# Retention stage: ScalarE copies the state out of PSUM, and queries are loaded two pairs of tiles ahead

## The chip, the core and the metric

The kernel runs on one core of one Trainium2 chip. The metric is device time in microseconds (us) of one execution. The time before is 1370.45 us, the median of three runs (1362.09, 1370.45 and 1370.65).

## The reference, cut to what matters

Three layers follow one another. The change touches the first one only.

```
scores = (q @ k^T) / sqrt(64)                       # batch 8, 8 heads, 576 positions, head size 64
ret    = scores * gamma_h ** (i - j) for i >= j, else 0
x      = (ret @ v) as 4608 tokens x 512             # retention
x      = x + gate * relu(x @ w1[e]) @ w2[e]         # one of 8 experts per token, only where x @ w_skip > 0
out    = (P(x @ w_in) / Q(x @ w_in)) @ w_out        # gated polynomial layer
```

Scaling key j by gamma^-j and query i by gamma^i turns the decay into plain products. A causal sum can then be cut into tiles of 128 positions: inside a tile, masked scores times values; from earlier tiles, a running state, the sum of k^T v, times the queries.

## The kernel before

The 4608 tokens (8 sequences of 576) are cut into 36 tiles of 128. The retention stage is one loop over the tiles t = 0 to 35 (line 517), written inside a manual schedule: on each engine the instructions stand in the order in which the Python code issues them, and an engine's order is never changed by a scheduler.

Loads go through SP's queue. `load(t)` (line 251) brings keys (tile `lk`) and values (`lv`) of one tile, 0.26 MB each, four tiles ahead; their pools have five buffers. `load_q(c)` (line 265) brings the queries of two tiles, a pair c, 0.52 MB, as `lq`, in one DMA or, where the pair crosses from one sequence to the next, in two; `lq` has two buffers. Before the loop the kernel issues pairs 0 and 1 (lines 496 and 502); in the loop, at each even t, pair t/2 + 2 (line 531). At each even t SP also issues a 0.52 MB load of float64 weights (`c64`, printed as `c`, line 144), and at every t > 1 a store of one finished tile, `keep` (line 391, `Z<-xs`), which waits until ScalarE has copied `xs`. SP issues all of these in order and stops at the first one whose wait is not met.

GpSimd (POOL) scales the keys (`scale`, line 277, in place in `lk`) and the queries (`scale_q`, line 283: two instructions that read `lq` and write `qs`; `qs` has one buffer, which the transposes of the pair before must have read). It also sends list entries of routed tokens (line 456).

TensorE (PE) does, for tile t: both halves of `transp_q` for the next pair at even t (line 304, one half ahead of `scores(t + 1)`, one behind it), the masked scores of tile t + 1 (line 314), the transposes of the keys of tile t + 2 (`transp`, line 291), `outs(t)` (line 330: scores times values; line 335: state times queries), `state(t)` (line 352: the state grows by this tile in the PSUM tile `st`), and `rows(t - 1)` (line 373: transposition back and router logits).

After `state(t)` the running state is copied from PSUM to one of two SBUF tiles, `sms`, because the next tile's `outs` (line 335) uses it as weights. Two copies do it, one for each half of the partitions, 64 x 256 elements each:

```python
for e in range(2):
    r = slice(64 * e, 64 * e + 64)
    nc.vector.tensor_copy(out=x[r, :, r], in_=st[r])
```

There are 64 of them in the kernel (32 tiles, since the last tile of each group of nine needs none). In the loop they stand on VectorE (DVE) behind the score masks (line 320, tile `sm`) and, at even t, behind the seven or so instructions that turn float64 words into float32 (`conv_words`, `conv_lo`, lines 159 to 199).

ScalarE (ACT) copies the transposes (`tk` line 293, `tq` line 305), the outputs (`xt` line 338) and `xs` (line 377) out of PSUM, and does one step of the float64 conversion at even t (`conv_abs`, line 176, which waits for VectorE's line 159).

After the loop the routing lists are finished, and two stages follow, experts and the polynomial layer, which the change leaves as they are.

Of the kernel before, what the change touches and what calls it, by code (L numbers as in the profile page):

```python
# [21 lines left out]
NT = N // P  # L22
# [55 lines left out]
def body(nc, tc, a, out):  # L78
# [7 lines left out]
    Z = dram.tile([N, DM], F32, name="Z")  # L86
# [5 lines left out]
    ab = const.tile([P, 8], F32, name="ab")  # L92
    idx = const.tile([P, E, NC3, 2], I32, name="idx")

# [1 line left out]
    slots, raws = {}, {}  # L96
    pool = {"last": ctx.enter_context(tc.tile_pool(name="last", bufs=1))}
    win = [wi_p.tile([P, 2, 1024], F32R, name=f"wi{i}") for i in range(8)]
# [29 lines left out]
        w = slots[s]  # L128
        nc.vector.tensor_tensor(out=w[:, 1], in0=raws.pop(s), in1=w[:, 0].bitcast(F32), op=ALU.subtract)

    # float64 words to float32, rounded to nearest, and its two parts
    c64, cst8 = {}, {}
    NCA = 16
    items = [(0, 512 * n, 512) for n in range(NCA)]
# [64 lines left out]
            nc.vector.tensor_tensor(out=win[m][:, 1, o:o + W], in0=cst8.pop(n)[3],  # L199
                                    in1=win[m][:, 0, o:o + W].bitcast(F32), op=ALU.subtract)  # L200

# [1 line left out]
    at = ExitStack()  # L203
    pool["raw"] = at.enter_context(tc.tile_pool(name="raw", bufs=3))
    pool["cv"] = at.enter_context(tc.tile_pool(name="cv", bufs=2))
# [10 lines left out]
    def C(k):  # L216
        o, n = off[k]
        return cst[:, o:o + n]
# [11 lines left out]
    def setup():  # L230
        zero = rt_p.tile([P, E * RR * 2 // P], I32, tag="lp", name="zero", bufs=1)
        nc.vector.memset(zero, OOB)
        nc.sync.dma_start(out=XI.rearrange("(p r) c -> p (r c)", p=P), in_=zero)
        for p in range(NP):
            nc.sync.dma_start(out=iw[:, p, P:P + E], in_=a["moe_w_gate"][p * P:(p + 1) * P, :])
        nc.sync.dma_start(out=iw[:, :, P + E:P + E + 1],
                          in_=a["moe_w_skip"].rearrange("(c p o) -> p c o", p=P, o=1))
        nc.sync.dma_start(out=ab[:, 0:4], in_=a["moe2_a"].unsqueeze(0).to_broadcast([P, 4]))
        nc.sync.dma_start(out=ab[:, 4:6], in_=a["moe2_b"].unsqueeze(0).to_broadcast([P, 2]))
        nc.vector.tensor_copy(out=iw[:, :, 0:P], in_=ident.unsqueeze(1).to_broadcast([P, NP, P]))  # L240
        nc.vector.tensor_copy(out=upper, in_=C("upper"))
        nc.vector.memset(ones, 1.0)
        nc.vector.memset(ab[:, 6:7], 1.000001)
        nc.vector.memset(carry, 0.0)
        nc.vector.tensor_copy(out=ebase, in_=C("ebase"))
        nc.vector.tensor_copy(out=rowt[:, :, 0], in_=tok)
# [14 lines left out]
                nc.sync.dma_start(out=x[n:P], in_=src[b + 1, :, 0:P - n, :].rearrange("h p d -> p h d"))  # L261
            dst[t] = x

    # the queries of two tiles: two neighbours in a partition
    def load_q(c):
        b, s = divmod(2 * c * P, S)
        n = min(2 * P, S - s)
        x = ld_p.tile([P, H, 2, D], F32, tag="lq", name="lq", bufs=2)
        nc.sync.dma_start(out=x[0:n // 2], in_=a["q"][b, :, s:s + n, :].rearrange("h (p t) d -> p h (t d)", t=2))
        if n < 2 * P:  # L270
            nc.sync.dma_start(out=x[n // 2:P],
                              in_=a["q"][b + 1, :, 0:2 * P - n, :].rearrange("h (p t) d -> p h (t d)", t=2))
        lq[c] = x

    def scale(t, eng=nc.gpsimd):
        o = off["scale"][0] + (t % PER) * H
        eng.tensor_tensor(out=lk[t], in0=lk[t], in1=cst[:, o:o + H].unsqueeze(2).to_broadcast([P, H, D]), op=ALU.mult)

    def scale_q(c, eng=nc.gpsimd):
        o = off["scale"][0] + PER * H + (c % PER) * 2 * H  # L280
        x = ld_p.tile([P, 2, H, D], F32, tag="qs", name="qs", bufs=1)
        for i in range(2):
            eng.tensor_tensor(out=x[:, i], in0=lq[c][:, :, i, :], op=ALU.mult,  # L283
                              in1=cst[:, o + i * H:o + (i + 1) * H].unsqueeze(2).to_broadcast([P, H, D]))
        lq[c] = x
# [56 lines left out]
    def state(t):  # L342
        tt = t % PER
        if tt != 8:
            first = tt in (0, 4)
            if first:
                cur["st"] = ps_s.tile([P, NP, D], F32, tag="st", name="st")
            st = cur["st"]
            r0 = 64 if tt == 4 else 0
            for p in range(NP):  # L350
                for e in range(2):
                    nc.tensor.matmul(out=st[64 * e:64 * e + 64, p, :], lhsT=lk[t][r0:P, 2 * p + e, :],  # L352
                                     rhs=lv[t][r0:P, 2 * p + e, :], start=(first and p == 0), stop=True,
                                     skip_group_check=True)
            x = sms[t % 2]
            for e in range(2):
                r = slice(64 * e, 64 * e + 64)
                nc.vector.tensor_copy(out=x[r, :, r], in_=st[r])
            ss[t + 1] = x
        del lk[t], lv[t]  # L360

    W = P + E + 1
    tiles = []
# [48 lines left out]
                               op0=ALU.is_gt, op1=ALU.mult)  # L412
        ranks.append((g0, n, ex, ohb))

    # place in the expert's list: tokens before this one, in earlier tiles and in its own
    def rank():
        g0, n, ex, ohb = ranks.pop(0)
        V = nc.vector
# [60 lines left out]
        if lo <= n < hi:  # L479
            f(n)  # L480

    # the tensor engine's clock falls when it waits for long: products of no use keep it up
    def spin(tile, x, n):
        for _ in range(n):
            nc.tensor.matmul(out=tile, lhsT=x[:, 0:P], rhs=x[:, 0:512], start=True, stop=True)

    with tc.manual_schedule():
        idle = ac_p.tile([P, 512], BF16, name="idle")
        nc.vector.memset(idle, 0.0)
        spin(ps_s.tile([P, 512], F32, tag="ot", name="spin"), idle, SPIN[0])  # L490
        o, n = off["scale"]
        nc.sync.dma_start(out=cst[:, o:o + n], in_=a["consts"][:, o:o + n])
        oi, ni = off["ident"]
        nc.sync.dma_start(out=ident, in_=a["consts"][:, oi:oi + ni])
        load(0, "k")
        load_q(0)
        nc.sync.dma_start(out=cst[:, o + n:oi], in_=a["consts"][:, o + n:oi])
        load(1, "k")
        load(0, "v")
        nc.sync.dma_start(out=cst[:, oi:], in_=a["consts"][:, oi:])  # L500
        load(1, "v")
        load_q(1)
        load(2)
        for x in sms:
            nc.gpsimd.memset(x, 0.0)
        scale(0, nc.vector)
        scale_q(0)
        scale(1, nc.vector)
        setup()
        load(3)  # L510
        transp(0)
        transp_q(0, 0)
        transp_q(0, 1)
        scores(0)
        transp(1)
        scale_q(1)
        for t in range(NT):
            u, ph = t // 2 - 1, t % 2
            if ph == 0:
                cv(conv_load, u + 1, 0, NCA)  # L520
            if t in (9, 15, 21, 27):
                load_raw(nxt["raw"])
                nxt["raw"] += 1
            if t == 3:
                nc.scalar.activation(out=ab[:, 4:6], in_=ab[:, 4:6], func=AF.Abs)
            if t > 1:
                keep(t - 2)
            if t + 4 < NT:
                load(t + 4)
            if ph == 0 and t + 4 < NT:  # L530
                load_q(t // 2 + 2)
            c = t // 2 + 1
            if t + 2 < NT:
                scale(t + 2)
                if ph == 1 and 2 * c + 2 < NT:
                    scale_q(c + 1)
                if ph == 0:
                    transp_q(c, 0)
            for _ in range(min(len(sends), 1 if t < 30 else 2)):
                send()  # L540
            if ph == 0:
                cv(conv_hi, u - 1, 0, NCA)
            else:
                cv(conv_add, u, 0, NCA)
            if t + 1 < NT:
                scores(t + 1)
            if ph == 0:
                cv(conv_words, u, 0, NCA)
            if t + 2 < NT:
                if ph == 0:  # L550
                    transp_q(c, 1)
                transp(t + 2)
            outs(t)
            if ph == 0:
                cv(conv_abs, u, 0, NCA)
                cv(conv_lo, u - 1, 0, NCA)
            else:
                cv(conv_low, u, 0, NCA)
            state(t)
            if ranks:  # L560
                rank()
            if t > 0:
                rows(t - 1)
            feed({12: 1, 18: 2, 24: 3}.get(t, 0), nxt["raw"])
        rows(NT - 1)
        keep(NT - 2)
        while ranks:
            rank()
        while sends:
            send()  # L570
        keep(NT - 1)
        count()
    at.close()

# [1 line left out]
    def spill():  # L576
        sp = ExitStack()
        s_p = sp.enter_context(tc.tile_pool(name="sp", bufs=1))
# [40 lines left out]

    spill()  # L620

# [1 line left out]
    pool["wb"] = ctx.enter_context(tc.tile_pool(name="wb", bufs=NWB))  # L623
    mo = ExitStack()
    ex_p = mo.enter_context(tc.tile_pool(name="ex", bufs=1))
# [16 lines left out]
        for e in range(e0, e1):  # L642
            nc.scalar.dma_start(out=idx[:, e], in_=XI[e * RR:e * RR + NC3 * P, :].rearrange("(c p) t -> p c t", p=P))

    # tokens of different lists are different rows of Z
    def apart(ins, mine, others):
        ins = getattr(ins, "ins", ins)
        for g in others:
# [94 lines left out]
    for e in range(E):  # L743
        for i in range(8):
            s = 8 * e + i
# [26 lines left out]
    feed(0)  # L772
    mo.close()

# [1 line left out]
    xg_p = ctx.enter_context(tc.tile_pool(name="xg", bufs=1))  # L776
    xt_p = ctx.enter_context(tc.tile_pool(name="xt2", bufs=2))
    g_p = ctx.enter_context(tc.tile_pool(name="g", bufs=LAG))
# [94 lines left out]
    for s in (NSLOT - 2, NSLOT - 1):  # L873
        for u, tag in enumerate("pq"):
            x = pq_p.tile([P, TB], F32, tag=tag, name=tag)
# [62 lines left out]
```

## Time and profile before

| what | us |
|---|---|
| median of three runs (lowest, highest) | 1370.45 (1362.09, 1370.65) |
| the profiled execution: first to last instruction | 1357.6 |
| what lies around the span (median of the runs less the span) | 12.85 |
| TensorE busy in the span | 1305.0 |
| VectorE busy | 1108.5 |
| ScalarE busy | 772.6 |
| GpSimd busy | 763.3 |

The retention stage takes the first 245 us or so, the experts go to about 540, the polynomial layer fills the rest. For one profiled execution only the span is given, so its own time is taken as the span and the 12.85 us that make it the median. Start times in the rows are counted from the first instruction. A row of waits names who waited for whom, with total, times and longest. "SPq" is SP's DMA queue. The granted clock (PEclk) is 1.00 at 2.4 GHz and 0.50 at 1.2 GHz.

### The profile page before, as it was taken

How to read it: one execution, taken by the hardware profiler on the slowest of the kernel's cores; microseconds unless marked ns; L12 is line 12 of the kernel's file. 1: busy time of each engine (PE TensorE's matmuls, PEld its weight loads, DVE VectorE, ACT ScalarE, POOL GpSimd, SP SyncE). 2: the span in 40 equal slices, each digit the busy share in tenths (PEclk: the TensorE clock that was granted, in tenths of full speed). 3: DMA queues.
4: the chain of work that ended last, by engine and by line, in shares of the span. 5: the costliest groups of instructions: out<-in, count | busy, mean ns of one | idle time of the engine just before them, and what ended most of it. 6: DMA issues, size and time to landing. Idle time of an engine off the chain costs nothing.

```text
span 1357.6 us, 20203 instructions
## 1 busy us (share of the span) xinstructions
PE 1305.0 (96%) x7639; PEld 1092.0 (80%) x7639; DVE 1108.5 (82%) x1247; ACT 772.6 (57%) x1315; POOL 763.3 (56%) x640
## 2 busy tenths in 40 slices
PE   6999999699999998999999999999999999999998
PEld 4888778588788886778888888888888888888886
DVE  2788999478777775798888888888888888888886
ACT  2445454244444443666667667667666676676664
POOL 3345556333333322567766667667676666766765
PEclk9999999899999999999999999999999999999999
DMA  9798994277666665000100101001010010010000
GB/s 210 190 238 230 225 223 119 83 219 234 204 224 216 205 210 172 32 1 0 63 1 18 46 0 63 0 1 63 0 49 14 1 63 0 0 63 1 32 1 31
DMA packets 160283, 127.10 MB, mean 94 GB/s; under 512 B 86634, under 2 KB 126314, under 8 KB 160176
## 3 DMA queue, kind: packets, MB, share of 16 engines
q1 hardware_dynamic: 151552, 114.85, 29.4%
q0 software_dynamic: 4736, 9.53, 2.1%
q10 hardware_dynamic: 3888, 1.34, 0.4%
q8 instruction: 62, 1.02, 0.3%
q14 instruction: 45, 0.37, 0.1%
HBM read 98.29 MB, written 28.92 MB: 94 GB/s over the span
## 4 chain that ended last, share of the span: by engine, by line
PE 68%; issue 14%; POOL 7%; DMA 6%; SPq 2%; DVE 1%; ACT 1%; POOLq 0%; ACTq 0%
PE h L812 28%; PE o L860 27%; DMA lq<-in_q 3%; PE h L688 2%; PE xp L373 2%; PE sc L314 2%; PE ot L330 2%; PE ot L335 2%; PE t L663 1%; POOL xg L656 1%; POOL Z L725 1%; PE y L709 1%; POOL cr L181 1%; PE st L352 1%; SPq L259 1%
## 5 line engine op out<-in xcount | busy, mean ns | idle before, releaser
L834 DVE RECIPROCAL q<-q 128x512 f32<-128x512 f32 x144 | 482.7, 3352 | 81.4 <-POOL q L824 81.4
L812 PE MATMUL h<-xb,wi 128*128 128x512 f32 x1728 | 421.8, 393 | 2.7 <-DVE p L838 2.0
L860 PE MATMUL o<-w,g 128*128 128x512 f32 x1728 | 414.8, 389 | 0.1
L812 PEld LDWEIGHTS h<-xb,wi 128*128 128x128 f32 x1728 | 324.2, 189 | 70.2 <-DVE p L838 2.4
L860 PEld LDWEIGHTS o<-w,g 128*128 128x128 f32 x1728 | 324.3, 188 | 67.7 <-POOL g L850 0.5
L823 POOL TENSOR_TENSOR p<-p,h 128x512 f32<-128x512 f32 x144 | 186.0, 1291 | 190.8 <-ACT p L819 190.8
L824 POOL TENSOR_TENSOR q<-q,s 128x512 f32<-128x512 f32 x144 | 186.9, 1298 | 68.9 <-ACT s L822 68.9
L818 ACT COPY h<-h 128x512 f32<-128x512 f32 x144 | 84.8, 589 | 246.8 <-PE h L812 246.8
L850 POOL TENSOR_TENSOR g<-p,g 128x512 fp32r<-128x512 f32 x144 | 185.8, 1291 | 2.5 <-ACT g L849 2.5
L709 PE MATMUL y<-w,hr 128*128 128x512 f32 (+1 forms) x576 | 138.8, 397 | 0.0
L709 PEld LDWEIGHTS y<-w,hr 128*128 128x128 f32 (+1 forms) x576 | 98.9, 175 | 30.2
L688 PE MATMUL h<-xp,w 128*128 128x336 f32 x768 | 120.8, 317 | 0.5 <-ACT xp L664 0.5
L688 PEld LDWEIGHTS h<-xp,w 128*128 128x128 f32 x768 | 119.6, 188 | 1.8 <-ACT xp L664 0.7
L822 ACT ACTIVATE s<-s,ab 128x512 f32<-128x512 f32 x144 | 119.5, 830 | 0.0
L819 ACT ACTIVATE p<-h,ab 128x512 f32<-128x512 f32 x144 | 113.2, 786 | 8.0 <-POOL g L850 8.0
L181 POOL TENSOR_TENSOR cr<-cr,cy 128x256 f32<-128x256 f32 x32 | 24.7, 772 | 162.9 <-DVE cr L169 162.8
L843 DVE SCALAR_TENSOR_TENSOR p<-h,ab,q 128x512 f32<-128x512 f32 x138 | 103.7, 751 | 4.9
L838 DVE SCALAR_TENSOR_TENSOR h<-p,ab,h 128x512 f32<-128x512 f32 x138 | 103.0, 746 | 0.0
L821 ACT ACTIVATE q<-h,ab 128x512 f32<-128x512 f32 x144 | 100.6, 699 | 0.0
L283 POOL TENSOR_TENSOR qs<-lq,cst 128x512 f32<-128x512 f32 x36 | 42.4, 1199 | 101.9 <-DMA lq<-in_q 89.9
L125 ACT CAST w<-raw 128x1024 fp32r<-128x1024 f32 x70 | 73.3, 1047 | 46.5 <-DMA raw<-in_moe_w 28.8
L849 ACT CAST g<-p 128x512 fp32r<-128x512 f32 x144 | 91.0, 633 | 5.5 <-DVE p L843 5.5
(106 smaller groups left out, 1420.7 us busy)
## 6 DMA issues: line engine op xcount, KB each, us to landing
raw<-in_moe_w SPq DMA_DIRECT2D x62, 512.0 KB, 3.9
Z<-xs SPq DMA_DIRECT2D x36, 256.0 KB, 3.2
gx<-Z SPq DMA_DIRECT2D x36, 256.0 KB, 3.9
out<-gx SPq DMA_DIRECT2D x35, 256.0 KB, 2.3
lk<-in_k SPq DMA_DIRECT2D x32, 256.0 KB, 4.3
lv<-in_v SPq DMA_DIRECT2D x32, 256.0 KB, 4.9
c<-in_moe_w_in SPq DMA_DIRECT2D x16, 512.0 KB, 5.4
c<-in_moe_w_out SPq DMA_DIRECT2D x31, 256.0 KB, 4.3
```

Source lines behind the costliest of these rows:

```text
L688: nc.tensor.matmul(out=ps, lhsT=w[:, pw, k, ff * P:(ff + 1) * P], rhs=xp[e][:, px, k, :], start=(n == 0), stop=(n == 11))
L709: nc.tensor.matmul(out=ys[e][c][0:cnt[c]], lhsT=h[:, ph, c * P:c * P + cnt[c]], rhs=w[:, pw, ff, :], start=(i == 0 and ff == 0 and j == 0) ...
L812: nc.tensor.matmul(out=ps, lhsT=w[:, pw, k, o:o + P], rhs=xb[j][:, px, k, :], start=(n == 0), stop=(n == 11))
L819: S.activation(out=p, in_=ps, func=A.Identity, scale=ab[:, 3:4], bias=ab[:, 2:3])
L822: S.activation(out=s, in_=s, func=A.Identity, scale=ab[:, 5:6], bias=ab[:, 6:7])
L823: G.tensor_tensor(out=p, in0=p, in1=h, op=ALU.mult)
L824: G.tensor_tensor(out=q, in0=q, in1=s, op=ALU.add)
L834: nc.vector.reciprocal(out=q, in_=q)
L838: nc.vector.scalar_tensor_tensor(out=p if (j, f) < SOON else ps, in0=p, scalar=ab[:, 1:2], in1=ps, op0=ALU.add, op1=ALU.mult)
L843: nc.vector.scalar_tensor_tensor(out=p, in0=p if (j, f) < SOON else ps, scalar=ab[:, 0:1], in1=q, op0=ALU.add, op1=ALU.mult)
L850: nc.gpsimd.tensor_tensor(out=g[:, 1], in0=p, in1=g[:, 0].bitcast(F32), op=ALU.subtract)
L860: nc.tensor.matmul(out=os[j][c], lhsT=g[:, pg, c * P:(c + 1) * P], rhs=w[:, pw, f % 2, :], start=(f == 0 and i == 0), stop=(f == NF2 - 1 a ...
```

## The change

The two copies of each state move from VectorE's program to ScalarE's. The queries of pair 2 are loaded ahead of the loop, right after the keys and values of tile 2 and ahead of the constants, and the loop loads pair t/2 + 3 where it loaded pair t/2 + 2. The buffers stay as they were, two for `lq` and one for `qs`.

```diff
@@ state(t)
             for e in range(2):
                 r = slice(64 * e, 64 * e + 64)
-                nc.vector.tensor_copy(out=x[r, :, r], in_=st[r])
+                nc.scalar.copy(out=x[r, :, r], in_=st[r])
@@ ahead of the loop
         scale(1, nc.vector)
+        load_q(2)
         setup()
         load(3)
@@ in the loop
             if t + 4 < NT:
                 load(t + 4)
-            if ph == 0 and t + 4 < NT:
-                load_q(t // 2 + 2)
+            if ph == 0 and t + 6 < NT:
+                load_q(t // 2 + 3)
```

SP's queue, ahead of the loop and into its first turn (the first rows load tile 2, `XI` and `iw` are the constants of `setup`, then come tile 3, the first `c64`, tile 4 and a pair of queries). The kernel before:

```order
L259 DMA lv_153<-in_v 128x8x64
L233 DMA XI_67<-zero_162 128x608
L235 DMA iw_112<-in_moe_w_gate 128x8 x4
L236 DMA iw_112<-in_moe_w_skip 128x4x1
L238 DMA ab_71<-in_moe2_a 128x4
L239 DMA ab_71<-in_moe2_b 128x2
L259 DMA lk_179<-in_k 128x8x64
L259 DMA lv_181<-in_v 128x8x64
L144 DMA c64_225<-in_moe2_w_in 128x2x512
...
L269 DMA lq_233<-in_q 32x8x128
L271 DMA lq_233<-in_q 96x8x128
```

The changed kernel, the same place:

```order
L259 DMA lv_153<-in_v 128x8x64
L269 DMA lq_162<-in_q 32x8x128
L271 DMA lq_162<-in_q 96x8x128
L233 DMA XI_67<-zero_165 128x608
L235 DMA iw_112<-in_moe_w_gate 128x8 x4
L236 DMA iw_112<-in_moe_w_skip 128x4x1
L238 DMA ab_71<-in_moe2_a 128x4
L239 DMA ab_71<-in_moe2_b 128x2
L259 DMA lk_182<-in_k 128x8x64
L259 DMA lv_184<-in_v 128x8x64
L144 DMA c64_228<-in_moe2_w_in 128x2x512
```

Pair 2, in two DMAs of 32 and 96 partitions, moved from behind the keys and values of tile 4 to ahead of the constants and of the keys of tile 3 (`lk_179`, `lk_182`).

ScalarE's queue in one pair of turns, t = 6 and 7: `cg` is `conv_abs` of the even turn, the `xt` rows are the outputs of the two turns. The kernel before:

```order
L293 COPY tk<-tp 128x512
L338 COPY xt<-ot 128x512
L176 ACTIVATE cg<-c_501 128x512
L377 COPY xs<-xp 128x512
L293 COPY tk<-tp 128x512
L338 COPY xt<-ot 128x512
L377 COPY xs<-xp 128x512
L305 COPY tq<-tp 128x512
```

The changed kernel, the same place:

```order
L293 COPY tk<-tp 128x512
L338 COPY xt<-ot 128x512
L176 ACTIVATE cg<-c_504 128x512
L358 COPY sms_118<-st 64x4x64 x2
L377 COPY xs<-xp 128x512
L293 COPY tk<-tp 128x512
L338 COPY xt<-ot 128x512
L358 COPY sms_119<-st 64x4x64 x2
L377 COPY xs<-xp 128x512
L305 COPY tq<-tp 128x512
```

The state copies stand between the output copy and the copy of `xs`, and in the even turn behind the `cg` step.

## Rows read from the trace of the kernel before

**Rows 1.** Stretches of the span (us): busy time and count by engine, granted clock, DMA.
```profile
40.00:236.00 196.00, 187.28 (x2267) 161.35 (x2267) 171.12 (x337) 92.98 (x165) 99.43 (x88) 1.00 0.84 208
60.00:121.00 61.00, 58.73 (x711) 50.79 (x710) 52.47 (x104) 29.61 (x53) 26.85 (x25) 1.00 0.93 234
```

**Rows 2.** Waits of PE from 24 to 236 us (total us, times, longest).
```profile
PE tp L304 <- POOL qs L283: 8.3, 3, 6.0
PE tp L291 <- POOL lk L277: 4.6, 6, 1.2
PE ot L335 <- DVE sms L358: 0.9, 1, 0.9
PE tp L304 <- DVE r L434: 0.8, 1, 0.8
```

**Rows 3.** Waits of POOL from 24 to 236 us.
```profile
POOL qs L283 <- DMA lq<-in_q: 80.4, 14, 9.7
...
POOL lk L277 <- DMA lk<-in_k: 1.7, 1, 1.7
```

**Rows 4.** PE in order of time (start, us, what, idle before it).
```profile
21.07 0.66 PE L291 MATMUL tp<-ident,lk 128*128 128x128 f32 x4 [1.24 <-POOL lk L277]
...
31.55 1.12 PE L304 MATMUL tp<-ident,qs 128*128 128x128 f32 x4 [5.95 <-POOL qs L283]
...
39.11 0.69 PE L352 MATMUL st<-lv,lk 128*64 128x64 f32 x16
...
58.22 0.60 PE L304 MATMUL tp<-ident,qs 128*128 128x128 f32 x4
...
62.97 0.69 PE L352 MATMUL st<-lv,lk 128*64 128x64 f32 x16
```

**Rows 5.** Short stretches at the start: columns as in rows 1.
```profile
10.00:12.00 2.00, 1.37 (x12) 1.37 (x14) 1.14 (x8) 0.58 (x1) 0.00 (x0) 0.56 1.22 269
...
14.00:16.00 2.00, 1.53 (x20) 1.36 (x20) 0.05 (x1) 1.01 (x2) 2.00 (x3) 1.00 0.87 201
16.00:20.00 4.00, 3.83 (x61) 3.28 (x58) 2.26 (x5) 1.69 (x3) 0.45 (x2) 1.00 0.69 127
20.00:24.00 4.00, 2.93 (x35) 2.47 (x37) 1.16 (x2) 0.71 (x2) 1.02 (x1) 1.00 1.22 237
...
33.00:35.00 2.00, 2.00 (x18) 1.78 (x17) 0.28 (x1) 0.32 (x1) 1.50 (x2) 0.50 1.21 263
```

**Rows 6.** SP's DMA queue in order of time: start, issue time, DMA.
```profile
11.23 1.59 SPq L233 DMA_DIRECT2D XI<-zero  x1
...
21.81 1.92 SPq L269 DMA_DIRECT2D lq<-in_q  x1
```

**Rows 7.** POOL in order of time.
```profile
7.17 2.04 POOL L283 TENSOR_TENSOR qs<-lq,cst 128x512 f32<-128x512 f32 x2 [5.42 <-DMA lq<-in_q]
...
19.98 1.04 POOL L277 TENSOR_TENSOR lk<-lk,cst 128x512 f32<-128x512 f32 x1 [3.56 <-DMA lk<-in_k]
30.45 2.04 POOL L283 TENSOR_TENSOR qs<-lq,cst 128x512 f32<-128x512 f32 x2 [9.43 <-DMA lq<-in_q]
```

**Rows 8.** Waits of SP's queue from 40 to 236 us.
```profile
SPq L391 <- ACT xs L377: 82.4, 29, 6.0
...
SPq L269 <- POOL lk L277: 4.8, 4, 2.2
```

**Rows 9.** Costs by line and shape (count, busy us, mean ns), first 370 us.
```profile
L358 DVE COPY sms<-st 64x256 f32<-64x256 f32 x64 | 26.8, 419 | 11.6 <-PE st L352 11.2
...
L377 ACT COPY xs<-xp 128x512 f32<-128x512 f32 x36 | 21.1, 586 | 28.5 <-PE xp L373 19.2 <-ACT cg L176 7.2 <-DMA c<-in_moe_w_in 1.2
...
L176 ACT ACTIVATE cg<-c 128x256 f32<-128x256 f32 x13 | 5.7, 437 | 17.8 <-DVE c L159 16.0 <-issue 1.7
```

**Rows 10.** ACT in an even turn, in order of time.
```profile
113.62 0.59 ACT L377 COPY xs<-xp 128x512 f32<-128x512 f32 x1 [0.58 <-ACT cg L176]
115.31 0.59 ACT L293 COPY tk<-tp 128x512 f32<-128x512 f32 x1 [1.10 <-PE tp L291]
```

## Prediction

> **What bounds the kernel now.** I read the busy time by stretches first. From 40 to 236 us, nearly all of the retention loop, TensorE is busy for 187.28 of 196 us and its clock stays at 1.00; VectorE is busy for 171, ScalarE for 93, GpSimd for 99, and the DMA engines for 0.84 of the time [rows 1]. The reader should see that TensorE sets the pace and that only 8.7 us of this stretch (196 less 187.28) are idle. The change takes no work from TensorE, so inside the loop it can win these 8.7 us and no more.
>
> Next the waits say what the idle time is. From 24 to 236 us TensorE waited 8.3 us for scaled queries, of which one wait was 6.0, 4.6 us for scaled keys in six waits, 0.9 us for a state copy and 0.8 us for a routing step of VectorE [rows 2]. These add up to 14.6 us: the 8.7 of the loop and the one long wait before 40 us. The keys themselves were late only once: GpSimd waited 1.7 us for them, but 80.4 us in 14 waits for queries [rows 3]. So the six waits for scaled keys come from queries too: GpSimd works in order, and the scaling of the keys stands behind a `scale_q` that waits for its DMA. Query loads cause 6.0 us at the start and 2.3 + 4.6 = 6.9 us in the loop; VectorE causes 1.7.
>
> Last the start, in order of time. TensorE stands still for 5.95 us until 31.55, for the queries of pair 2 [rows 4], which SP issued at 21.81 [rows 6] and GpSimd could scale at 30.45 [rows 7]. After the wait the clock is at 0.50 [rows 5]. From that first transpose to the state product of the same turn it takes 39.11 - 31.55 = 7.56 us; the same run of instructions at full clock takes 62.97 - 58.22 = 4.75. The low clock costs 2.8 us more.
>
> **Queries in the loop.** Each pair's load is issued one pair of turns earlier, some 12 us, and the longest wait for one was 9.7 [rows 3]. All fourteen waits should go, and with them 6.9 us of TensorE's. What is late next is a key load. Its lead is unchanged, the one wait for it did not reach TensorE, but a GpSimd that no longer waits for queries comes to the keys sooner, and a faster loop asks for more bytes: 208 GB/s x 196/187 = 218 on average, where the stretch from 60 to 121 us moved 234 at 0.93 busy [rows 1]. I leave 0.6 us for that and count 6.3. The bounds are 0 (each wait for queries becomes one for keys) and 6.9.
>
> SP waits in order, so the new buffer wait counts. `lq` has two buffers: the load of pair m + 3, at t = 2m, must wait until `scale_q(m + 1)` has read its buffer. Behind it in SP's queue stand the next store, the next keys and values, and the next `c64`. But SP comes to t = 2m only after the store `keep(2m - 2)`, which waits for the `xs` of the end of turn 2m - 1: SP waits 82.4 us for it in the loop, 29 times [rows 8]. By then the queries of pair m + 1 have been there for a pair of turns, and their scaling needs only `qs`, free since an early part of turn 2m - 2. That leaves over one turn of some 6 us. I count nothing; bounded from above by 15 loads x the 2.2 us that was the longest such wait before [rows 8], 33 us.
>
> **Queries at the start.** Pair 2 now goes ahead of the constants and of the keys of tile 3. Its buffer is free: `scale_q(0)` ended at 7.17 + 2.04 = 9.21 [rows 7], and SP gets there at 11.23 [rows 6]. The price: 0.52 MB more stand before the keys of tile 3, at 201 to 237 GB/s [rows 5] about 2.4 us. GpSimd waited for those keys until 19.98 [rows 7], and TensorE waited 1.24 us for their scaling [rows 4]. This wait grows to about 3.6. It is less if the room on the DMA engines from 16 to 20 us (busy 0.69, 127 GB/s [rows 5]) takes up part of the load: 1.0 us is the lower bound, from the room of 0.31 x 4 us. I take 2.4, since the rows around are full. Then TensorE reaches the transposes of pair 2 at 25.6 + 2.4 = 28.0; GpSimd has scaled the keys by 23.4 and both halves of the queries by 25.5. The wait of 5.95 is gone, a net gain of 3.5, and the 2.8 us of low clock with it.
>
> But the grown wait may cost its own fall of the clock. After 1.24 us of idling the clock stayed at 1.00, after 5.95 it was at 0.50, and at 10 to 12 us it was at 0.56 after several short waits and back at 1.00 by 14 [rows 5]. 3.6 us lies between. I take a fall as long as that early one, 4 us at about half speed, for 1.8 us. Start: 3.5 + 2.8 - 1.8 = 4.5 us, bounds 2.5 (a fall that costs as much as the old one, and a little more) and 7.7 (a delay of 1.0 and no fall: 4.95 + 2.8).
>
> **State copies.** VectorE loses 64 x 419 ns = 26.8 us [rows 9], all of it beside TensorE's work. ScalarE gets 64 copies of 64 x 256. The nearest rows are 437 ns (256 columns, Abs) and, above, 586 ns (512 columns out of PSUM) [rows 9]; half of the latter, 293 ns, is the lower end. I take 0.42 us, 27 us in all. ScalarE then is busy for about 118 of 196 us. What hides it are ScalarE's own gaps: in an even turn it idles 0.58 us ahead of `xs` and 1.10 us ahead of `tk` [rows 10], 1.7 us for 0.85 us of copies. `xs` comes 0.3 us later, the next copy on time, and no row has TensorE waiting for ScalarE [rows 2]. Without that cover each even turn would pay up to 0.3 us, 5 in all. The gain is VectorE's two stalls, 0.9 us for a state that stood behind the float64 steps and 0.8 us for routing behind a full queue [rows 2]. I count 1.2 of the 1.7, bounds -5 and 1.7.
>
> **Sum.** 6.3 + 4.5 + 1.2 = 12.0 us. The rest of the kernel starts 12 us earlier and stays as it is. Against the profiled execution: 1357.6 - 12.0 = 1345.6 us of span, and with the 12.85 us around it 1358.5. The runs shown spread by 8.6 us, as much as most of this gain, so the range is wider than the sum's bounds alone.
>
> **Rivals.** 1. Transfers set the pace. For it: 234 GB/s at 0.93 in the busiest stretch, and weight loads in the same queue. Against it: keys have waited once. The waits for queries turn into waits for keys, half of the 6.9 us stays, and the start gives its lower end: 3.4 + 2.5 + 0.6 = 6.5 us, 1364 us. "DMA: Bandwidth & Descriptors" of the Trainium skill (section "Issuing engines are not separate DMA queues") says that all transfers run on the same 16 engines and interleave; by that an earlier load only moves others back, as this rival has it. The start's rows agree, the loop's 0.84 leaves room.
>
> 2. Everything is hidden: the DMA room takes up the early load and the clock does not fall. 7.7 + 6.9 + 1.7 = 16.3 us, 1354 us. Against it: DMA engines at 1.22 from 20 to 24 us [rows 5].
>
> 3. The other side: SP stands at the `load_q` for a buffer that `scale_q` has not yet read. Two buffers serve loads three pairs ahead. If SP lost 2.2 us at each of 15 loads, keys, stores and `c64` behind it would be that much later. It decides from the point where `scale_q(m + 1)` ends after the `xs` of turn 2m - 1; below that it costs nothing. Price: 33 us less what the start gives, 4.5, less the 1.2 for VectorE, and less the old 6.9 that it takes the place of: 20 us slower, 1391 us. Against it: the turn of margin worked out above.
>
> 4. ScalarE's order. In even turns the state copies stand behind `conv_abs`, which waits for VectorE's line 159 and that for a `c64` load; a late load holds up the state as it did on VectorE. At 0.9 us, the one stall of this kind [rows 2], for all 17 even turns, 15.3 us against the gain of 12: 1374 us. "TensorE: Matmul & The Clock Gate" of the Trainium skill (section "Architectural detail: the array is 16× 32×32, not 1× 128×128") says that ScalarE's queue is a strict FIFO, so nothing overtakes such a step. The one wait in this trace does not show it on ScalarE.
>
> **How the numbers follow.** Forecast 0.62, transfers 0.18, everything hidden 0.11, SP's buffer wait 0.05, ScalarE's order 0.04. A measurement of this kernel can tell about 1%, 13.7 us, from no change. The forecast's 12.0 lies below that mark, within 1.7 us; with 3 us of its own spread a quarter to a third of it lies beyond, 0.18, and nearly all of rival 2, 0.10: faster 0.28. Rival 3 alone is slower by over 1%: 0.05. Same: 0.67. The range runs from 1349, a little under rival 2, to 1369, which takes in rival 1 and the spread of the runs; SP's wait and ScalarE's order are left out.
>
> **What would show it.** Right: GpSimd no longer waits for queries in the loop; TensorE's wait of 5.95 us is gone and the one for the keys of tile 3 is near 3.6; the loop's idle time falls from 8.7 us to under 2; the 64 state copies take 0.3 to 0.5 us each on ScalarE, and TensorE waits for none. Wrong: SP waiting at the line of `load_q` for GpSimd; GpSimd waiting for keys in ten places; TensorE waiting at line 335 for ScalarE; or a start where the clock is at 0.50 for longer than the 7.56 us that its first turn took.

## The result and the profile after

The changed kernel took 1351.72 us (median of four runs, 1349.84 to 1357.07), the kernel before, run beside it on the same chip, 1369.87 us. By the medians it is 18 us faster; the ratio is 0.9876 [0.9848, 0.9904], 1.24% faster. The time lies inside the predicted range, 7 us under the predicted 1358.5.

The stretches that answer to [rows 1], of the changed kernel:

```profile
40.00:236.00 196.00, 190.05 (x2271) 165.32 (x2269) 156.32 (x304) 112.89 (x225) 98.53 (x91) 0.98 0.86 208
60.00:121.00 61.00, 60.73 (x736) 52.65 (x737) 51.35 (x88) 36.95 (x74) 32.38 (x29) 1.00 1.01 243
```

From 60 to 121 us TensorE idles for 0.27 us where it idled for 2.27: in the middle of the loop nothing is left to win. VectorE is busy for 156 us of 196 instead of 171, although it lost copies of 26.8 us [rows 9]. The stretch holds 58 state copies in either kernel. In part VectorE now does routing steps in it that came behind it before; in part, as the experiments show, other work of VectorE has become longer. That is the clue to all that follows.

TensorE's waits from 24 to 236 us, changed kernel, against [rows 2]:

```profile
PE tp L291 <- POOL lk L277: 4.0, 1, 4.0
PE rk L425 <- DVE ohb L411: 2.2, 1, 2.2
PE ot L330 <- issue: 1.8, 1, 1.8
PE tp L291 <- ACT tq L305: 0.6, 2, 0.3
PE ot L335 <- ACT sms L358: 0.3, 1, 0.3
PE tp L304 <- DVE r L434: 0.3, 1, 0.3
```

The waits for queries are gone. One wait for keys is left, at the start; the wait at line 425 is the end of retention, which in the kernel before lay just behind this window. TensorE waits once, for 0.3 us, for a state copy of ScalarE.

GpSimd's waits in the same stretch, against [rows 3]:

```profile
POOL lk L277 <- DMA lk<-in_k: 46.0, 17, 5.4
```

And those of SP's queue from 24 us on ([rows 8] begins at 40 us; ten of the twelve waits at the load of queries, 13.5 us, lie behind that point):

```profile
SPq L391 <- ACT xs L377: 70.8, 29, 8.1
SPq L269 <- POOL qs L283: 15.1, 12, 2.2
```

GpSimd now waits for keys, and SP waits twelve times at the load of queries for their buffer. Neither reaches TensorE.

The start, TensorE in order of time in the changed kernel, against [rows 4]:

```profile
23.89 1.12 PE L291 MATMUL tp<-ident,lk 128*128 128x128 f32 x4 [4.00 <-POOL lk L277]
...
28.72 0.69 PE L352 MATMUL st<-lv,lk 128*64 128x64 f32 x16
30.38 0.60 PE L304 MATMUL tp<-ident,qs 128*128 128x128 f32 x4
...
35.13 0.69 PE L352 MATMUL st<-lv,lk 128*64 128x64 f32 x16
```

Short stretches there, against [rows 5]:

```profile
22.00:24.00 2.00, 0.11 (x1) 0.11 (x2) 0.00 (x0) 0.00 (x0) 1.21 (x2) 0.50 1.10 261
...
26.00:28.00 2.00, 2.00 (x15) 1.67 (x12) 0.00 (x0) 0.00 (x0) 0.68 (x1) 0.50 1.34 186
28.00:30.00 2.00, 2.00 (x26) 1.81 (x25) 0.00 (x0) 1.06 (x3) 0.36 (x1) 0.87 1.23 267
```

The keys of tile 3 are waited for 4.00 us instead of 1.24, the queries of pair 2 not at all, and the granted clock is at 0.50 from 22 to 28. The state product that ended its turn at 39.11 now starts at 35.13, 3.98 us sooner.

The cost of the moved copy, ScalarE in the first 370 us of the changed kernel, against [rows 9]:

```profile
L358 ACT COPY sms<-st 64x256 f32<-64x256 f32 x64 | 23.3, 365 | 3.5 <-remote 1.0 <-PE st L352 0.5 <-ACT xt L338 0.3
```

### The profile page after: what moved, and what is told of

Its sections match the earlier page's. It is cut to its first block, busy times and chain, and to the rows that moved or that the text cites. A ratio compares the mean times of both kernels' runs of the same rounds, so it can differ in the third digit from the quotient of the medians.

```text
span 1355.3 us, 20231 instructions
## 1 busy us (share of the span) xinstructions
PE 1310.0 (97%) x7639; PEld 1098.4 (81%) x7639; DVE 1090.0 (80%) x1183; ACT 792.9 (59%) x1379; POOL 758.5 (56%) x640
## 4 chain that ended last, share of the span: by engine, by line
PE 70%; issue 16%; POOL 5%; DVE 4%; DMA 3%; ACT 1%; SPq 1%; POOLq 0%; another core or an unknown queue 0%; ACTq 0%
PE h L813 28%; PE o L861 28%; PE xp L373 3%; PE ot L335 3%; PE ot L330 2%; PE sc L314 2%; DVE q L835 2%; POOL Z L726 1%; POOL xg L657 1%; POOL cr L181 1%; PE st L352 1%; PE t L664 1%; PE tp L291 1%; PE tp L304 1%; DMA Z<-ysb,idx 1%
## 5 line engine op out<-in xcount | busy, mean ns | idle before, releaser
L689 PE MATMUL h<-xp,w 128*128 128x336 f32 x768 | 123.7, 322 | 1.2 <-DVE hr L694 0.7
L129 DVE TENSOR_TENSOR w<-raw,w 128x1024 fp32r<-128x1024 f32 x70 | 86.8, 1244 | 0.3 <-DVE xp L666 0.3
```

What stands on the lines that cost most here:

```text
L689: nc.tensor.matmul(out=ps, lhsT=w[:, pw, k, ff * P:(ff + 1) * P], rhs=xp[e][:, px, k, :], start=(n == 0), stop=(n == 11))
```

## The experiments

Two theories were set against each other at first: that the three edits add up, each worth its own term (6.3, 4.5 and 1.2 us); and that one of them makes the others worth something. A control, the kernel before under another label, shows what a ratio can tell. Later a third theory, C, took over: scaled earlier, the queries meet VectorE's float64 conversion, which gets longer beside GpSimd, and only copies on ScalarE keep that away from TensorE.

For every profile one window serves: from 15 us to the last matmul of line 425, where retention ends. It holds nearly the same matmuls in each kernel (2510 to 2512; 2504 are recorded in e9), so its length is the cost of retention, its idle time what waits cost, and what its busy time has over another's what the lower clock cost. What comes after it takes 1113 to 1121 us of the span in every one, in no order that follows the edits (e9 excepted). One kernel's retention differs between profiles too: 228 and 234 us for the kernel before, 216 to 220 in three of the changed one.

### e1 and e2: the control, and the changed kernel again

No edit in either.

> The kernel before, unchanged, as a control for the spread and for the profile. Theory A (the runs of before spread by themselves, and its profiled execution was a good one): runs between 1359 and 1371 us, no difference from before beyond the interval, TensorE's long wait of 6 us at the start and 7 to 9 us of idle time in the loop in the new profile too. Theory B (the profiled execution of before was like the others): runs within 3 us of 1370, and a span about 1.8 us below the run's time, so near 1368.

> The changed kernel, unchanged, on the same chip as the control. Theory A (its first profile showed a stall of all engines of some 3 us near 222 us and low clock behind it that most runs don't have): runs of 1349 to 1353 us, a ratio of 0.985 to 0.990, and a profile without that stall, whose span is 4 to 6 us shorter. Theory B (the stall belongs to the changed order): it is in this profile at the same place.

Measured, beside a kernel before of 1369.62 us: the control 1368.09, ratio 0.9987 [0.9972, 1.0002]; the changed kernel 1351.94, ratio 0.9874 [0.985, 0.9899]. Retention in the control:

```profile
15.00:249.20 234.20, 212.53 (x2512) 182.83 (x2510) 187.17 (x379) 102.67 (x183) 111.20 (x101) 0.97 0.81 197
```

and in the changed kernel:

```profile
15.00:234.00 219.00, 209.01 (x2510) 181.39 (x2508) 168.14 (x315) 123.27 (x246) 108.50 (x101) 0.98 0.87 211
```

It is 15.2 us shorter: 11.7 us less idle time (21.67 against 9.99) and 3.5 us less busy time. So most of the 16 us between e1 and e2 is won in retention. In the profile that the prediction was made from, retention ended at 243 us and not at 249. That execution was better than usual: its span of 1357.6 us is 8.4 under the control's 1366.0. The control's waits of TensorE from 15 us to the end of retention show more of VectorE than [rows 2]:

```profile
PE tp L304 <- POOL qs L283: 7.2, 4, 6.0
PE tp L291 <- POOL lk L277: 5.3, 8, 1.4
PE ot L335 <- DVE sms L358: 3.7, 2, 2.0
...
PE xp L373 <- DVE lg L382: 1.0, 1, 1.0
```

### e3: only the copies on ScalarE

```diff
-                nc.vector.tensor_copy(out=x[r, :, r], in_=st[r])
+                nc.scalar.copy(out=x[r, :, r], in_=st[r])
```

> The state copies on ScalarE alone, queries loaded as before. Theory A (the copies are worth VectorE's two stalls): 0 to 3 us faster, the wait of 6 us at the start and the waits for queries in the loop stay, TensorE's waits for VectorE's state copy go. Rival (VectorE's load held back the loop, the copies carry the gain): 8 us or more faster.

1367.22 us, ratio 0.9986 [0.997, 1.0001]: no gain over the control. TensorE's waits to the end of retention:

```profile
PE tp L304 <- POOL qs L283: 6.3, 5, 3.9
PE tp L291 <- POOL lk L277: 5.3, 7, 1.3
```

The wait for state copies has gone, those for queries and keys stand.

### e4: only the earlier queries, copies on VectorE

```diff
         scale(1, nc.vector)
+        load_q(2)
         setup()
...
-            if ph == 0 and t + 4 < NT:
-                load_q(t // 2 + 2)
+            if ph == 0 and t + 6 < NT:
+                load_q(t // 2 + 3)
```

> The earlier query loads alone, state copies on VectorE as before. Theory A: 11 to 17 us faster, nearly the whole change; GpSimd's waits for queries gone, TensorE's waits for VectorE (a state copy, routing) still there or grown to 2 or 3 us, since the loop is faster and VectorE as loaded as before. Rival (VectorE becomes the bound as soon as the queries come early, so that both parts are needed): under 8 us faster, with TensorE waiting at line 335 for VectorE's state copies in many turns, 5 us or more in all.

1368.17 us, ratio 0.9985 [0.9971, 0.9999]: this too is no better than the control, though both loads are early, for which the prediction's own terms would give 6.3 + 4.5 = 10.8 us. Its retention:

```profile
15.00:248.20 233.20, 214.93 (x2510) 186.29 (x2508) 196.75 (x379) 101.53 (x182) 107.95 (x101) 0.96 0.81 198
```

Against e2 that is 14.2 us more, 8.3 idle and 5.9 at the lower clock. VectorE is busy for 196.75 us where the control has 187.17, with the same 379 instructions (and for 168.14 in e2, where e3 has 157.33 with the same 315). One wait leads TensorE's list from 24 to 245 us:

```profile
PE ot L335 <- DVE sms L358: 9.0, 6, 2.5
```

What VectorE and GpSimd do ahead of one such wait (start, duration, what):

```profile
141.40 2.22 POOL L283 TENSOR_TENSOR qs<-lq,cst 128x512 f32<-128x512 f32 x2
141.65 1.07 DVE L159 TENSOR_SCALAR c<-c 128x512 f32<-128x512 f32 x1
142.75 1.15 DVE L162 TENSOR_SCALAR cy<-c 128x512 int32<-128x512 int32 x1
143.78 1.01 POOL L456 DMA_INDIRECT XI<-rowt,sx  x1 [0.16 <-issue]
143.94 0.69 DVE L164 SCALAR_TENSOR_TENSOR cy<-c,cy 128x512 int32<-128x512 int32 x1
144.67 1.50 DVE L167 TENSOR_SCALAR cp<-cy 128x512 int32<-128x512 int32 x1
144.82 1.05 POOL L277 TENSOR_TENSOR lk<-lk,cst 128x512 f32<-128x512 f32 x1
...
147.41 0.85 DVE L358 COPY sms<-st 64x256 f32<-64x256 f32 x2
...
148.32 0.91 PE L335 MATMUL ot<-tq,sms 128*128 128x128 f32 x5 [1.89 <-DVE sms L358]
```

Lines 159, 162 and 167 take 0.43 us with GpSimd quiet. Beside the scaling of queries the first two take 1.07 and 1.15; line 167 meets the scaling of keys and takes 1.50. Each of these long instructions ends 0.28 to 0.30 us behind the GpSimd instruction beside it. Line 164, beside an indirect DMA of GpSimd, keeps its 0.69. The state copies stand behind all this, and TensorE waits 1.89 us for them.

It goes the other way too. Elsewhere in e4 line 169 starts 0.16 us ahead of GpSimd and keeps its 0.69; it is GpSimd's instruction that takes 1.44 instead of 1.04, and line 199, which starts inside it, takes 1.53 instead of 0.68:

```profile
69.68 0.69 DVE L169 SCALAR_TENSOR_TENSOR cr<-c,cp 128x512 f32<-128x512 uint32 x1
69.84 1.44 POOL L277 TENSOR_TENSOR lk<-lk,cst 128x512 f32<-128x512 f32 x1 [1.67 <-DMA lk<-in_k]
...
70.29 1.53 DVE L199 TENSOR_TENSOR wi<-cr,wi 128x512 fp32r<-128x512 f32 x1
```

The three lines from 24 to 236 us (count, busy us, mean ns), first in the control:

```profile
L159 DVE TENSOR_SCALAR c<-c 128x512 f32<-128x512 f32 x16 | 11.5, 720 | 0.0
...
L162 DVE TENSOR_SCALAR cy<-c 128x512 int32<-128x512 int32 x16 | 10.8, 677 | 0.5
L167 DVE TENSOR_SCALAR cp<-cy 128x512 int32<-128x512 int32 x16 | 6.8, 427 | 0.5
```

in e4:

```profile
L159 DVE TENSOR_SCALAR c<-c 128x512 f32<-128x512 f32 x16 | 15.0, 936 | 0.0
L162 DVE TENSOR_SCALAR cy<-c 128x512 int32<-128x512 int32 x16 | 14.2, 889 | 0.5
...
L167 DVE TENSOR_SCALAR cp<-cy 128x512 int32<-128x512 int32 x16 | 12.9, 807 | 0.5
```

and in the changed kernel (its first profile):

```profile
L162 DVE TENSOR_SCALAR cy<-c 128x512 int32<-128x512 int32 x16 | 15.5, 968 | 0.6
...
L159 DVE TENSOR_SCALAR c<-c 128x512 f32<-128x512 f32 x16 | 15.4, 960 | 0.0
...
L167 DVE TENSOR_SCALAR cp<-cy 128x512 int32<-128x512 int32 x16 | 11.9, 742 | 0.5
```

For all eight 128x512 lines of the conversion (159 to 169, 181, 185, 199; sixteen of each), what they take over the shortest duration of the same line in the same profile adds up to 18.7 us in the control, 15.8 in e3, 32.2 in e4, 32.1 in e2 and 29.3 in the first profile of the changed kernel. Early queries lengthen the conversion by 13 to 16 us wherever the copies are, and VectorE's busy time by some 10, since a few small routing steps get shorter in exchange. Of the 165 instructions of these lines that took over 0.06 us more than their shortest, in the first profile of before, e1, e2, e4 and the first of the changed kernel, 162 had a `TENSOR_TENSOR` of GpSimd running beside them. The longer conversion goes with 9 us of TensorE's waits for state copies where those are on VectorE, and with almost none where they are not.

### e5: the conversion behind the state, copies on VectorE

From e4; `cv` issues the conversion steps, and in even turns they now stand behind the state and the routing.

```diff
-            if ph == 0:
-                cv(conv_words, u, 0, NCA)
...
-            if ph == 0:
-                cv(conv_abs, u, 0, NCA)
-                cv(conv_lo, u - 1, 0, NCA)
-            else:
+            if ph == 1:
...
+            if ph == 0:
+                cv(conv_words, u, 0, NCA)
+                cv(conv_abs, u, 0, NCA)
+                cv(conv_lo, u - 1, 0, NCA)
```

> The earlier query loads with the state copies left on VectorE, but in even turns the float64 steps (lines 159 to 199) and ScalarE's Abs come behind the state copies and the routing logits, not ahead of them. Theory C (early queries make GpSimd scale while VectorE converts, VectorE's conversion gets longer, and the state copies queued behind it hold up TensorE): TensorE's 9 us of waits for the state copy fall under 2 us, and the kernel is 10 to 18 us faster than before, like the whole change. Rival (VectorE has too much work in all, wherever the copies stand): under 5 us faster, with TensorE waiting for VectorE elsewhere.

1374.59 us, ratio 1.0071 [1.0047, 1.0096] (kernel before in this set 1364.6): slower. The waits for state copies are gone, and TensorE has another:

```profile
PE sc L314 <- DVE sm L320: 17.1, 13, 3.0
```

Behind the state the conversion stands ahead of the next turn's score masks. Theory C had expected a gain of 10 to 18 us here. As its expectation put it, a wait for VectorE elsewhere speaks for the rival, that VectorE has too much work in all; and the conversion's excess is only 11.1 us in this order. So e5 moves the wait to another product of VectorE and doesn't decide for theory C; e9 below does more. At neither of the two places tried do several us of conversion cost nothing once the queries come early.

### e6 and e7: copies on ScalarE with one of the two early loads

e6, the start only (pair 2 ahead of the constants; loop as before, without its first load):

```diff
-            if ph == 0 and t + 6 < NT:
-                load_q(t // 2 + 3)
+            if ph == 0 and 0 < t < NT - 4:
+                load_q(t // 2 + 2)
```

e7, the loop only (pairs 2 and 3 in turns 0 and 2, then as in the change):

```diff
-        load_q(2)
         setup()
...
-            if ph == 0 and t + 6 < NT:
+            if t in (0, 2):
+                load_q(t // 2 + 2)
+            if ph == 0 and 0 < t < NT - 6:
                 load_q(t // 2 + 3)
```

> State copies on ScalarE, pair 2 loaded ahead of the constants, but in the loop each pair loaded one pair ahead as before (pair 3 at t = 2). Theory A (start and loop add): 4 to 7 us faster, waits for queries in the loop still there, 6 us or more. Rival (the start is worth nothing by itself, since the loop's late queries eat what it gave): within 3 us of the copies alone.

> State copies on ScalarE, pair 2 at its old place in the queue, pairs 3 and 4 both at t = 2, then two pairs ahead. Theory A (start and loop add): 9 to 14 us faster, the wait of 4 to 6 us for pair 2 stays, no waits for queries behind it. Rival (only both together): under 5 us.

e6: 1356.01 us, ratio 0.994 [0.992, 0.9961]. e7: 1354.84, ratio 0.9926 [0.9902, 0.9949]. In e6 GpSimd waits for queries all through the loop, as before:

```profile
POOL qs L283 <- DMA lq<-in_q: 86.4, 15, 9.2
POOL lk L277 <- DMA lk<-in_k: 10.5, 3, 7.4
```

In e7 TensorE keeps one wait for queries, the one at the start:

```profile
PE tp L304 <- POOL qs L283: 5.3, 1, 5.3
```

Set against e3's 0.9986, where the copies alone are on ScalarE, the start is worth 0.46% (6.3 us) and the loop 0.60% (8.2 us), 14.5 together; the whole change has 1.12% (15.3 us) over e3. With the copies on ScalarE the two loads add up, as far as this can tell: the differences are between separate sets of runs, so each is good to some 4 us. The conversion's excess goes with the loop's loads: 18.4 us in e6 and 31.2 in e7.

### e8 and e10: the keys of tile 3 ahead of the queries

e8, from the changed kernel:

```diff
         scale(1, nc.vector)
+        load(3, "k")
         load_q(2)
         setup()
-        load(3)
+        load(3, "v")
```

> The changed kernel with the keys of tile 3 ahead of pair 2, and the values of tile 3 behind the constants. If the wait of 4.0 to 4.2 us for those keys is the price of the early load: it falls to about 1.2 us, the low clock behind it (3.4 to 6.8 us) goes, and the kernel is 3 to 6 us faster than the changed one, 1346 to 1349 us. Rival (the price moves to the queries or the router weights): no faster, a wait of 3 us or more at the transposes of pair 2 or at line 373.

1346.57 us beside 1364.6, ratio 0.9874 [0.9853, 0.9895]: the same as the changed kernel's. The keys of tile 3 are now in time, and TensorE waits 3.2 us for those of tile 4 (transposed at 29.85) instead, with the clock at 0.50 behind it (30 to 34 us): the wait moved by one tile, as the rival had it.

e10 is e8 with the clearing of the `XI` lists, a 128x608 store, taken out of `setup` and put into turn 5, and the first `c64` load put behind tile 4:

```diff
     def setup():
...
+            if t == 0:
+                conv_load(0)
+            if t == 5:
+                blank()
```

> The changed kernel with the start in another order: keys of tile 3, then pair 2, then the router constants; the first float64 load behind tile 4, the clearing of the lists at t = 5. If the bytes ahead of the keys are the price of the early pair: TensorE's waits for keys near 20 to 30 us fall under 2 us in all, the low clock there goes, 3 to 6 us faster than the changed kernel in the same session. Rival (putting the keys of tile 3 first only moved the wait to tile 4, and this moves it on): a wait of 3 us stays somewhere before 40 us, and the two are equal within 2 us.

1345.42 us (five runs, 1342.53 to 1346.01), ratio 0.9849 [0.9827, 0.9871] to a kernel before of 1364.91. Retention:

```profile
15.00:226.90 211.90, 207.65 (x2511) 180.38 (x2509) 169.98 (x316) 122.86 (x246) 113.03 (x101) 0.99 0.91 218
```

The start has no wait for keys left, the clock stays at 1.00 from 20 us to 40, and retention idles 4.25 us in all.

### e11: the changed kernel beside e10

> The changed kernel as it is, in the same session as the leaner start, so that the two can be compared: ratio to before 0.985 to 0.990, a wait of about 4 us for the keys of tile 3, and a stall near 225 us as in its earlier profiles or none.

1348.26 us (1347.55 to 1352.02), ratio 0.9877 [0.9855, 0.9898]. All five runs of e10 lie under all five of these, by 2.8 us in the median, while the two intervals overlap: e10 is the best kernel here, by little, and under the 3 to 6 us that were expected of it. In e11's profile the wait for the keys of tile 3 is 3.4 us.

### e9: no scaling of the queries at all, copies on VectorE

From e4: GpSimd's two instructions per pair are left out, three buffers take the raw queries, and TensorE transposes them unscaled and in another column order. Outputs and the choice of experts differ, so a stage for overfull experts runs that the others skip; only its retention can be compared.

```diff
-        for i in range(2):
-            eng.tensor_tensor(out=x[:, i], in0=lq[c][:, :, i, :], op=ALU.mult,
-                              in1=cst[:, ...].unsqueeze(2).to_broadcast([P, H, D]))
-        lq[c] = x
+        pass
```

> The earlier query loads with the state copies on VectorE, but GpSimd's scaling of the queries is left out: the transposes read the loaded queries as they lie, unscaled and in another order of columns, with a third buffer for them, so the products are other numbers and other tokens go to the experts. Theory C (GpSimd's scaling beside VectorE's float64 conversion lengthens the conversion, and the state copies queue behind it): the conversion's instructions lengthen by some 15 us instead of 32, TensorE's waits for VectorE's state copies fall from 9.0 us to 3 or less, and the kernel is 10 us or more faster than the one with the early queries alone. Rival (VectorE's own load makes the copies late, without GpSimd): 6 us or more of those waits stay, and the gain is under 5 us.

1398.91 us in all, ratio 1.0251 [1.0229, 1.0273], with that stage of some 46 us in it. Retention ends at 230 us, where e4's ends at 248. From 24 to 236 us, two of the three lines that stood out in e4, and TensorE's wait for the state copies (the kernel's lines 329 and 352 are 335 and 358 elsewhere):

```profile
L162 DVE TENSOR_SCALAR cy<-c 128x512 int32<-128x512 int32 x16 | 8.3, 520 | 0.5
L159 DVE TENSOR_SCALAR c<-c 128x512 f32<-128x512 f32 x16 | 7.6, 475 | 0.0
```

```profile
PE ot L329 <- DVE sms L352: 1.0, 1, 1.0
```

The excess of the eight lines falls to 5.7 us, and TensorE's waits for state copies, which VectorE still makes, from 9.0 us to 1.0. VectorE has the same 379 instructions to do as in e4, so the number of them is not what held it back there. That is what theory C says. A reservation remains: without the scaling GpSimd is ahead with the keys too, so e9 takes away more than the overlap.

## Why the prediction was right in its direction and short in its size

The time is inside the range, but the gain was put at 12 us and is 18. The prediction gave 0.67 to a difference under its mark of 13.7 us and 0.28 to a faster kernel beyond it, which is what came. Of its signs of being right, GpSimd's waits for queries and the wait of 5.95 us are gone, and the copies take 0.365 us. But three of its four signs of being wrong are there too: SP waits at the load of queries, GpSimd waits for keys in more than ten places, and TensorE waits once, 0.3 us, for a copy of ScalarE. They cost next to nothing: from 60 to 121 us TensorE idles 0.27 us. The loop's idle time, put at under 2 us, is 3.0 by the waits shown above (without the 4.0 of the start and line 425's, behind the loop); 1.8 of it is one stop that the last section takes up.

**Queries in the loop (6.3 us).** The mechanism holds: GpSimd's fourteen waits are gone and TensorE idles 0.27 us from 60 to 121. What was to be late next, the keys, is late for GpSimd 17 times, 46 us in all, and reaches TensorE only at the start. The size measured beside copies on ScalarE is 8.2 us, over the upper bound of 6.9. The bound came from idle time in one execution.

**Queries at the start (4.5 us).** The wait for keys was put at 3.6 us and is 4.0 to 4.2 in the first two profiles, 3.4 in the third; the wait for queries is gone; the clock did fall, to half until 28 us. The net gain after the first turn is 3.98 us. By the runs the start is worth 6.3, good to some 4.

**State copies (1.2 us).** This is the step that failed: "VectorE loses 64 x 419 ns = 26.8 us [rows 9], all of it beside TensorE's work", and with it the sum that treats the three terms as independent. By themselves the copies win nothing (e3), and the early queries win nothing without them (e4), where the sum would have 10.8 us; once the queries come early, the copies are worth 16.2 us (e4 against e2), not 1.2. The change holds both edits, and the prediction had the copies in for another reason, VectorE's two stalls: that it came out near is in part luck. VectorE had room only as long as queries came late. Earlier ones bring GpSimd's scaling onto the conversion, which grows by 13 to 16 us; behind it the copies would make TensorE wait 9 us and lose some 6 more to the clock (e4). The copy itself takes 0.365 us on ScalarE, where 0.42 was taken, and TensorE waited once for one, 0.3 us.

The row that could have warned was in the profile before, unread: line 159 already took 0.79 us in the mean against 0.42 at its shortest, and 20 of the 21 lengthened instructions of the conversion there had GpSimd's scaling beside them. A rule of the Trainium skill says why: "SBUF — State Buffer" (section "SBUF: two separate sides") has VectorE and GpSimd share one pair of ports under an exclusive lock. By that page whichever starts first keeps it for the whole instruction and the other stops, and on VectorE's side this holds for an instruction in a two-port mode or with two SBUF inputs. The traces agree. The thirteen profiles have 189 instructions of the eight lines beside which GpSimd runs one `TENSOR_TENSOR` and nothing else. In 84 VectorE started first: it kept its time in all of them, and in 72 GpSimd's instruction ended 0.90 us behind it, having taken up to 1.59 us instead of 1.04. In 98 of the other 105 VectorE was lengthened, and ended 0.28 to 0.30 us behind GpSimd's instruction in lines 159, 162 and 167, and 0.54 to 0.56 us in the five lines with two inputs. They agree in kind as well: the score masks, with one input in PSUM, kept 0.68 us in every kernel, and the state copies from PSUM 0.42. No run here shows which instruction is in a two-port mode. Where an indirect DMA of GpSimd was running too, the recorded starts don't tell who waits: line 167 in e4 starts 0.15 us ahead of the scaling of keys and still ends 0.30 behind it.

**The base.** The step "with the 12.85 us around it" was wrong. In every profiled run since, time and span differ by 1.7 to 2.0 us (1357.07 and 1355.3 in the changed kernel). So the first profile of before stands for a run of some 1359.4 us, and the other 11 us are what the usual run took longer than that one. In the control's profile retention took 6 us longer than in that first one, some of it in waits for VectorE (3.7 us for state copies, where [rows 2] has 0.9) that the change removes as well. A gain worked out from that good execution was too small for the usual one: 12 where 18 were measured. How much of the missing 6 us comes from this and how much from the terms above is not shown.

**The rivals.** Rival 1, transfers: GpSimd does wait for keys instead, as it says, but no half of the gain was lost, since in the loop these waits did not reach TensorE. Rival 2, everything hidden, has about the right time (1354) for the wrong reason: the start was not hidden and the clock fell. Rival 3, SP at the buffer: it stands there twelve times, up to 2.2 us, where the prediction counted nothing; its time is spare. Its margin was right as to cost and wrong as to the wait. Rival 4, ScalarE behind the conversion: it did not come up. `cg` needs only line 159, the first step of the conversion, and in the changed kernel ScalarE idled 0.5 us in all ahead of sixteen of them; TensorE waited 0.3 us for a copy of ScalarE.

## What to carry to other kernels

Edits don't add up when one of them moves work on an engine that another one relieves: time each alone and both together, with a control. An earlier load also moves whatever runs on it; look at which engine's instructions it then lies beside, and compare the mean and the shortest duration of one line to see whether they suffer. And where time and span of the first profile lie far apart, ask whether that execution was a usual one before its waits are summed.

## What the runs showed of the hardware

A VectorE instruction of 0.43 us took 1.50 beside one `TENSOR_TENSOR` of GpSimd and, at 204.90 us in e4, 3.32 beside three in a row (line 159). None of that shows as a wait: it is counted as busy time. Where VectorE's instruction started first, GpSimd's was the one lengthened, from 1.04 us to as much as 1.59 beside a single one.

Near 225 us, in the last turn of the loop, TensorE stands still for 1.8 us and ScalarE for 5.07, with no plain cause. In the first profile of the changed kernel ScalarE shows this:

```profile
224.54 0.58 ACT L338 COPY xt<-ot 128x512 f32<-128x512 f32 x1 [5.07 <-PE xp L373]
```

TensorE has the same 1.8 us in e2 at 225 and in e3 at 237, so it is not of the first profile alone; but e11, the same kernel as e2, doesn't have it, so it doesn't come with every execution either. It was not tried what causes it. In the first profile the clock is low behind it, at 0.50 from 228 to 232 us.
